# Pooled attention and MLP on one core: pooling of the first group on TensorE, smaller pieces of w_in, gelu over two blocks

## The chip, the cores and the metric

The kernel runs on one core of one Trainium2 chip. The metric is device time in microseconds (us) of one execution. A core has five engines, each with its own queue that it works off in order: TensorE (PE, matmuls and transposes into PSUM; its weight loads are shown as PEld), VectorE (DVE), ScalarE (ACT), GpSimd (POOL) and SyncE (SP, which here issues the loads and stores). PSUM holds what PE writes.

## The reference

```python
q, k, v: (8, 8, 576, 64)            # batch, heads, tokens, head_dim
k_p = k.reshape(B, H, 72, 8, 64).mean(axis=3)     # 8 tokens pooled into one
v_p = v.reshape(B, H, 72, 8, 64).mean(axis=3)
attn = softmax(q @ k_p.T / sqrt(64))
x = (attn @ v_p).transpose(0, 2, 1, 3).reshape(4608, 512)
h = x @ w_in                         # 512 x 2048
out = gelu_tanh(h) @ w_out           # 2048 x 512
```

## The kernel before, in words

The 4608 rows of x are worked off in nine groups of 512: one for each batch (its first 512 tokens) and one, R, for the last 64 tokens of all eight batches. The order is batches 0 to 6, R, batch 7. A group goes through attention and then the MLP; while PE runs one group's MLP, the attention of the next is slipped in between its matmuls.

**Layout.** K and V of a batch are 9 chunks of 128 pooled rows (`NB`): chunks 0 to 3 are K, chunk 4 is half K and half V, 5 to 8 are V. `pool` (L122) adds 8 float rows in three DVE instructions; `dup_k` (L139) writes the K result twice side by side. `pool_v_pe` (L132) does the sum on PE instead, as eight matmuls with a float identity accumulated in PSUM, and a copy. `k_transpose_pe` and `k_spread` (L171, L181) bring pooled K into `kbd`, block-diagonal by pairs of heads; `spread_v` (L143) multiplies pooled V by a mask into `vbd`. q is cast to bf16 (`cast_q`), transposed four head pairs at a time into `qT` (`q_transpose_pe`, L190).

**A block.** A group has four blocks j of 128 rows. `scores` (L202) makes 8 x 72 scores of a block in a "sc" tile, `exps` (L218) takes the exponential on ACT, `norm` (L225) sums, inverts and multiplies into `eb`; `e_transpose_pe` or a DMA transpose brings it into `eT`, and `values` / `values_half` (L259, L249) give xT. In group R each row belongs to another batch in its half of 64 rows, so `scores` uses two matmuls per head pair there, each for 64 rows of output.

**MLP.** `hidden` (L292) does one block of 128 hidden columns: 4 matmuls over k (`KO`), then a gelu on ACT into `gT`. `output` (L300) is one matmul of the second product; 16 (`FO`) make one 128-row block of the result, which `finish` copies and stores. In `mlp` a hidden block has all 512 rows; in `mlp_first`, for group 0, it has 256 (`half`), so that the work can begin with two blocks of attention done.

**Order.** Everything is written out by hand: an engine's queue has the order of the program text. The runner `hook(s)` calls functions at step s of an MLP; a step is one matmul (0 to 63, or 0 to 127 in `mlp_first`, for w_in; then 64 for w_out). The start, L361 to L471, is straight text: loads on SP, warm-up matmuls on PE (`warm_up`, L407), then pooling, scores, values of blocks 0 and 1 and scores of 2 and 3. Weights land as float in slots of the three-slot pool `kvp` that K and V use as well, and are cast to bf16 (`cast_w_in`, `cast_w_out`). PSUM tiles come from two rings, "mm" (4 of one bank) and "sc" (2 of two banks); a new tile waits until the reader of the one before it in its place is done.

Of the kernel before, what the change touches and what calls it, by code (L numbers as in the profile page):

```python
# [19 lines left out]
def kernel(  # L20
# [55 lines left out]
    def copy(eng, out, in_):  # L76
        if eng is nc.scalar:
            eng.copy(out=out, in_=in_)  # L78
        else:
            eng.tensor_copy(out=out, in_=in_)  # L80
# [41 lines left out]
    def pool(b, c0, c1):  # L122
        if "kvb" not in st[b]:
            st[b]["kvb"] = work.tile([128, NB, 2, D], BF16, name="kvb")
        t = st[b]["kv"][:, c0:c1]
        kvb = st[b]["kvb"]
        add = nc.vector.tensor_tensor
        add(out=t[:, :, 0:4, :], in0=t[:, :, 0:4, :], in1=t[:, :, 4:8, :], op=ALU.add)  # L128
        add(out=t[:, :, 0:2, :], in0=t[:, :, 0:2, :], in1=t[:, :, 2:4, :], op=ALU.add)  # L129
        add(out=kvb[:, c0:c1, 0, :], in0=t[:, :, 0, :], in1=t[:, :, 1, :], op=ALU.add)  # L130

    def pool_v_pe(b, c0, c1, eng):  # L132

        ps = psum.tile([128, 2, D], F32, name="vp", tag="mm", bufs=4)
        for i in range(8):
            nc.tensor.matmul(out=ps, lhsT=identf, rhs=st[b]["kv"][:, c0:c1, i, :], start=(i == 0), stop=(i == 7))
        copy(eng, st[b]["kvb"][:, c0:c1, 0, :], ps)

    def dup_k(b, c0, c1):  # L139
        kvb = st[b]["kvb"]  # L140
        nc.vector.tensor_copy(out=kvb[:, c0:c1, 1, :], in_=kvb[:, c0:c1, 0, :])
# [60 lines left out]
    def scores(g, j):  # L202
        sc = psum.tile([128, 2, MAIN], F32, name="sc", tag="sc", bufs=2)
        qT = st[g]["qT"]
        for pr in range(HP):
            o = sc[:, pr // 2, 2 * Sp * (pr % 2):2 * Sp * (pr % 2) + 2 * Sp]
            if g < B:
                nc.tensor.matmul(out=o, lhsT=qT[:, j, pr, :], rhs=kbd[:, g, pr].rearrange("d hh s -> d (hh s)"),  # L208
                                 start=True, stop=True)
            else:  # L210
                for half in range(2):
                    p0 = 64 * half
                    nc.tensor.matmul(out=o[p0:p0 + 64], lhsT=qT[:, j, pr, p0:p0 + 64],  # L213
                                     rhs=kbd[:, 2 * j + half, pr].rearrange("d hh s -> d (hh s)"),
                                     start=True, stop=True)
        st[g][("sc", j)] = sc
# [8 lines left out]
    def norm(g, j, eng):  # L225
        e = st[g][("e", j)]
        den = work.tile([128, H], F32, name="den")
        nc.vector.reduce_sum(out=den, in_=e, axis=AX.X)  # L228
        r = work.tile([128, H], F32, name="r")
        nc.vector.reciprocal(out=r, in_=den)  # L230
        eng.tensor_tensor(out=eb[:, j, 128 * 5 - W:].rearrange("p (h s) -> p h s", s=Sp), in0=e,  # L231
                          in1=r.unsqueeze(2).to_broadcast([128, H, Sp]), op=ALU.mult)
# [4 lines left out]
    def e_transpose_pe(g, j, eng):  # L237
        tp = psum.tile([128, 5, 128], BF16, name="tp", tag="mm", bufs=4)
        for c in range(5):
            nc.tensor.transpose(out=tp[:, c, :], in_=eb[:, j, 128 * c:128 * c + 128], identity=identb)  # L240
        copy(eng, st[g]["eT"][:, j], tp)
# [7 lines left out]
    def values_half(g, half, x, eng):  # L249

        xo = psum.tile([128, 2, 256], F32, name="xo", tag="mm", bufs=4)
        for i in range(2):
            pr = 2 * x + i
            for y, (c, n) in enumerate(PARTS[pr]):
                nc.tensor.matmul(out=xo[:, i, :], lhsT=vbd[:, g, n, :],  # L255
                                 rhs=st[g]["eT"][:, 2 * half:2 * half + 2, c, :], start=(y == 0), stop=(y == 1))
        copy(eng, st[g]["xT"][:, 2 * x:2 * x + 2, 256 * half:256 * half + 256], xo)
# [34 lines left out]
    def hidden(g, fo, c0, c1, hook, s):  # L292
        hp = psum.tile([128, MAIN], F32, name="mm", tag="mm", bufs=4)
        for ko in range(KO):
            hook(s + ko)
            nc.tensor.matmul(out=hp[:, 0:c1 - c0], lhsT=w_in_b[:, ko, fo * 128:(fo + 1) * 128],  # L296
                             rhs=st[g]["xT"][:, ko, c0:c1], start=(ko == 0), stop=(ko == KO - 1))
        nc.scalar.activation(out=gT[:, fo, c0:c1], in_=hp[:, 0:c1 - c0], func=ACT.Gelu_apprx_tanh)  # L298
# [10 lines left out]
    def mlp(g, hooks, last):  # L309
        hook = runner(hooks)  # L310
        for fo in range(FO):
            hidden(g, fo, 0, MAIN, hook, 4 * fo)
# [22 lines left out]
    def mlp_first(g, hooks):  # L335
# [3 lines left out]
        for half, c in [(0, 0), (0, 1), (0, 2), (0, 3), (1, 0), (1, 1), (1, 2), (1, 3)]:  # L339
            for fo in range(4 * c, 4 * c + 4):  # L340
                hidden(g, fo, 256 * half, 256 * half + 256, hook, s)
                s += 4
# [30 lines left out]
    for c in range(2):  # L373
        t = kvp.tile([128, KO, 1024], F32, name="w_in_s", tag="kv")
        w_in_s.append(t)
        for i in range(2):
            nc.sync.dma_start(
                out=t[:, :, 512 * i:512 * i + 512],
                in_=moe_w_in[:, 1024 * c + 512 * i:1024 * c + 512 * i + 512].rearrange("(ko p) f -> p ko f", p=128))

    def cast_w_in(c, eng):
        o = 512 * c
        copy(eng, w_in_b[:, :, o:o + 512], w_in_s[c // 2][:, :, 512 * (c % 2):512 * (c % 2) + 512])
# [9 lines left out]
    def cast_w_out(c, eng):  # L393
        copy(eng, w_out_b[:, 4 * c:4 * c + 4, :], w_out_s[c // 2][:, 4 * (c % 2):4 * (c % 2) + 4, :])

    make_identity(nc, identb)
    nc.vector.memset(kbd, 0.0)
# [7 lines left out]
    make_identity(nc, identf)  # L405
# [7 lines left out]
    warm_up(44, "mm")  # L413
    kT_tile(0, "mm")
    pool(0, 0, 2)
    dup_k(0, 0, 2)
    k_transpose_pe(0, 0, 2)
    pool(0, 2, 4)
    dup_k(0, 2, 4)
    warm_up(22, "mm")  # L420
    k_transpose_pe(0, 2, 4)
    pool(0, 4, 5)
    dup_k(0, 4, 5)
    warm_up(22, "mm")
    k_transpose_pe(0, 4, 5)
    k_spread(0, [nc.vector, nc.scalar])
# [3 lines left out]
    warm_up(12, "mm")  # L430
# [3 lines left out]
    q_transpose_pe(0, 1, nc.scalar, "mm")  # L434
    warm_up(4, "sc")
# [3 lines left out]
    pool(0, 5, 7)  # L439
    spread_v(0, nc.gpsimd, (0,))  # L440
    pool_v_pe(0, 7, 9, nc.scalar)
    spread_v(0, nc.gpsimd, (1,))
    cast_q(0, 2, 4, nc.gpsimd)
    spread_v(0, nc.gpsimd, (2,))
    warm_up(8, "mm")
    norm(0, 0, nc.vector)
    norm(0, 1, nc.vector)
    e_transpose_pe(0, 0, nc.scalar)
    q_transpose_pe(0, 2, nc.scalar, "mm")
    q_transpose_pe(0, 3, nc.scalar, "mm")  # L450
    e_transpose_pe(0, 1, nc.vector)
    cast_w_in(0, nc.vector)
    scores(0, 2)
    exps(0, 2)
    values_half(0, 0, 0, nc.vector)
    scores(0, 3)
    exps(0, 3)
    values_half(0, 0, 1, nc.scalar)
    nc.scalar.preload_act_table_set(GELU_SET)
    norm(0, 2, nc.gpsimd)  # L460
    cast_w_in(1, nc.vector)
    norm(0, 3, nc.vector)
    cast_w_in(2, nc.gpsimd)

    def first_t(j):
        e_transpose_pe(0, j, nc.vector)

    def first_v():
        cast_w_in(3, nc.vector)
        values_half(0, 1, 0, nc.scalar)  # L470
        values_half(0, 1, 1, nc.vector)  # L471
# [10 lines left out]
    load_main(1, "v", 0, 4, nc.sync)  # L482
# [10 lines left out]
    def at(hooks, s, f, *a):  # L493
        hooks.setdefault(s, []).append(lambda: f(*a))  # L494
# [7 lines left out]
    hooks = {}  # L502
    at(hooks, 16, first_t, 2)
    at(hooks, 32, first_t, 3)
    at(hooks, 42, first_v)
    at(hooks, 66, pool, 1, 0, 4)
    at(hooks, 66, dup_k, 1, 0, 4)
    at(hooks, 66, pool, 1, 4, 5)
    at(hooks, 66, dup_k, 1, 4, 5)
    at(hooks, 80, cast_q, 1, 0, 2, nc.vector)  # L510
    at(hooks, 80, cast_q, 1, 2, 4, nc.vector)
    at(hooks, 96, kT_tile, 1, "sc")
    at(hooks, 96, qT_tile, 1)
    at(hooks, 96, k_transpose_pe, 1, 0, 5)
    at(hooks, 96, k_spread, 1, [nc.vector, nc.vector])
    for j in range(4):
        at(hooks, 104 + 6 * j, q_transpose_pe, 1, j, nc.vector, "sc")
    at(hooks, 122, eT_tile, 1)
    at(hooks, 122, cast_w_out, 0, nc.vector)
    at(hooks, 122, cast_w_out, 1, nc.gpsimd)  # L520
    for j in range(4):
        at(hooks, [126, 127, 136, 140][j], scores, 1, j)
        at(hooks, [128, 128, 136, 140][j], exps, 1, j)
        at(hooks, [136, 140, 144, 148][j], norm, 1, j, nc.vector)
        at(hooks, [136, 140, 144, 148][j], e_transpose_dma, 1, j)
    at(hooks, 141, cast_w_out, 2, nc.scalar)
    at(hooks, 141, cast_w_out, 3, nc.scalar)
# [3 lines left out]
    at(hooks, 150, q_tile, 2)  # L531
    at(hooks, 150, load_q, 2, 0, 4, nc.sync)
    at(hooks, 150, load_kv, 2)
    tail_of_attention(hooks, 1, 187)
    mlp_first(0, hooks)

    for n_, g in enumerate(seq):
# [3 lines left out]
        if n_ + 1 < len(seq):  # L541
# [7 lines left out]
            if kv:  # L549
                t0 = 20 if n_ == 1 else 12  # L550
# [59 lines left out]
```

The softmax here doesn't subtract the row's maximum and nothing guards it: scores larger than these inputs give would overflow.

## Time and profile before

| what | value |
|---|---|
| median of 3 runs | 301.0 us (301.0 to 301.05) |
| profiled execution | 301.36 us, its span 299.3 us |
| PE busy | 290.7 us, 97% of the span, 1734 matmuls |
| ACT, DVE, POOL busy | 158.2, 146.7, 55.5 us |
| matmuls on w_out (L301) / on w_in (L296) | 128.6 / 127.6 us |
| gelu (L298) | 88.4 us in 160 instructions |
| K landed, first 512 KB | 4.20 us |
| first matmul on w_in / on w_out | 19.26 / 38.70 us |
| DMA engines, busy share from 5 to 45 us | 1.05 to 1.10 |

How to read the profile: times are from the start of the span. An instruction group has a line (L80 and L78 are the helper `copy` on DVE and ACT, so the tile's name tells what is copied), engine, operation, out<-in, shape and count. A bracket such as `[0.51 <-DMA w_in_s]` is the idle time of the engine just before, and what ended it. Matmuls are pipelined: a group's time runs from its first start to its last end. "The chain" follows the work that ended last back to the start; its last column is us, what. An engine's busy share over the span says little about the first 40 us, which differ from the rest.

### The profile page before, as it was taken

What the parts mean: (1) busy time and instruction counts of PE and PEld (TensorE: products, weight loads), DVE (VectorE), ACT (ScalarE), POOL (GpSimd) and SP (SyncE); (2) the same over time, 40 slices, a digit from 0 to 9 for tenths busy, and PEclk for the clock granted to TensorE, in tenths of its full rate; (3) what the DMA queues carried; (4) which work ended last, traced back from release to release, by engine and by line L of the source; (5) the groups of instructions that cost most, each with busy time, mean ns of one, the idle gap of its engine ahead of it and who ended that gap; (6) DMA issues with size and microseconds to landing.
All of it is one profiled execution on the core that took longest, in us unless ns stands there. A gap on an engine that the chain in (4) does not pass through costs nothing.

```text
span 299.3 us, 4581 instructions
## 1 busy us (share of the span) xinstructions
PE 290.7 (97%) x1734; PEld 151.6 (51%) x1734; DVE 146.7 (49%) x241; ACT 158.2 (53%) x242; POOL 55.5 (19%) x71
## 2 busy tenths in 40 slices
PE   7869999999999999999999999999999999999996
PEld 7748844445444544454445444544444544444444
DVE  6895769164706570648073807381639100920012
ACT  1477783667157715672477246724773267426500
POOL 3252033230400240024012400240024000100000
PEclk9999999999999999999999999999999999999999
DMA  7999997995699459947993599049944800351012
GB/s 235 357 387 338 384 350 132 343 279 158 135 279 250 145 127 271 269 146 126 261 297 134 119 249 301 4 107 249 276 147 101 164 36 2 79 114 37 0 70 70
DMA packets 73221, 56.32 MB, mean 188 GB/s; under 512 B 45808, under 2 KB 55408, under 8 KB 73200
## 3 DMA queue, kind: packets, MB, share of 16 engines
q1 hardware_dynamic: 73056, 55.98, 68.2%
q8 instruction: 13, 0.21, 0.3%
q10 hardware_dynamic: 144, 0.07, 0.1%
q14 instruction: 8, 0.07, 0.1%
HBM read 36.70 MB, written 9.44 MB: 154 GB/s over the span
## 4 chain that ended last, share of the span: by engine, by line
PE 91%; DMA 3%; DVE 2%; SPq 1%; POOL 1%; issue 0%; POOLq 0%
PE mm L296 41%; PE mm L301 41%; PE xo L266 4%; DMA q_sb<-in_q_dram 3%; PE sc L208 2%; PE mm L329 1%; POOL eb L231 1%; SPq L98 1%; PE xo L272 1%; PE tp L193 1%; PE sc L213 0%; DVE w_in_b L80 0%; PE tp L240 0%; DVE w_out_b L80 0%; POOL q_b L80 0%; PE xo L255 0%
## 5 line engine op out<-in xcount | busy, mean ns | idle before, releaser
L301 PE MATMUL mm<-w_out_b,gT 128*128 128x512 bf16 x560 | 128.6, 379 | 0.5 <-DVE w_out_b L80 0.5
L296 PE MATMUL mm<-xT,w_in_b 128*128 128x512 bf16 (+1 forms) x640 | 127.6, 358 | 0.5 <-DVE xT L80 0.5
L298 ACT ACTIVATE gT<-mm 128x512 bf16<-128x512 f32 (+1 forms) x160 | 88.4, 555 | 47.0 <-PE mm L296 45.9
L296 PEld LDWEIGHTS <-w_in_b 128*128 128x128 bf16 x640 | 62.2, 98 | 62.6 <-issue 0.5
L301 PEld LDWEIGHTS <-gT 128*128 128x128 bf16 x560 | 53.4, 98 | 59.7 <-DVE w_out_b L80 0.7
L80 DVE COPY osb<-mm 128x512 f32<-128x512 f32 (+2 forms) x37 | 24.3, 658 | 62.9 <-PE mm L301 60.8
L78 ACT CAST xT<-xo 128x1024 bf16<-128x1024 f32 (+1 forms) x18 | 16.6, 966 | 56.8 <-PE xo L266 49.1
L228 DVE TENSOR_REDUCE den<-e 128x8 f32<-128x576 f32 x36 | 26.5, 736 | 38.0 <-ACT e L221 37.9
L148 POOL TENSOR_TENSOR vbd<-kvb,vmask 128x256 bf16<-128x256 bf16 (+2 forms) x40 | 21.2, 553 | 113.5 <-DVE kvb L130 113.4
L128 DVE TENSOR_TENSOR kv<-kv 128x1024 f32<-128x1024 f32 (+3 forms) x20 | 22.4, 1118 | 29.7 <-DMA kv<-in_v_dram 27.7
L231 DVE TENSOR_TENSOR eb<-e,r 128x576 bf16<-128x576 f32 x28 | 27.2, 970 | 1.0
L221 ACT ACTIVATE e<-sc 128x576 f32<-128x576 f32 x36 | 22.5, 650 | 9.6 <-ACT e L221 4.0
L231 POOL TENSOR_TENSOR eb<-e,r 128x576 bf16<-128x576 f32 x8 | 10.1, 1266 | 71.5 <-ACT e L221 41.1
L80 POOL CAST q_b<-q_sb 128x2048 bf16<-128x2048 f32 (+1 forms) x7 | 15.0, 2147 | 4.1 <-DMA q_sb<-in_q_dram 4.1
L208 PEld LDWEIGHTS <-qT 128*128 128x128 bf16 x128 | 10.1, 98 | 7.0 <-ACT qT L78 0.6
L208 PE MATMUL sc<-kbd,qT 128*128 128x144 bf16 x128 | 13.2, 226 | 0.2 <-ACT qT L78 0.2
L266 PE MATMUL xo<-eT,vbd 128*128 128x512 bf16 x56 | 13.2, 379 | 0.0
L129 DVE TENSOR_TENSOR kv<-kv 128x512 f32<-128x512 f32 (+3 forms) x20 | 12.8, 640 | 0.7
L410 PE MATMUL warm<-identb 128*128 128x128 bf16 x112 | 9.1, 249 | 1.4 <-POOL vmask L398 1.4
L494 ACT ACT_TABLE_LOAD x8 | 10.3, 1283 | 0.1
L80 DVE COPY kbd<-kTd 64x288 bf16<-64x288 bf16 x12 | 5.6, 467 | 8.3 <-DMA kTd<-kvb 8.2
L314 ACT ACT_TABLE_LOAD x7 | 9.0, 1283 | 0.1
(55 smaller groups left out, 99.5 us busy)
## 6 DMA issues: line engine op xcount, KB each, us to landing
out_dram<-osb SPq DMA_DIRECT2D x31, 256.0 KB, 6.7
kv<-in_k_dram SPq DMA_DIRECT2D x7, 1024.0 KB, 6.5
q_sb<-in_q_dram SPq DMA_DIRECT2D x7, 1024.0 KB, 5.9
kv<-in_v_dram SPq DMA_DIRECT2D x7, 1024.0 KB, 9.9
w_in_s<-in_moe_w_in_dram SPq DMA_DIRECT2D x4, 1024.0 KB, 13.0
w_out_s<-in_moe_w_out_dram SPq DMA_DIRECT2D x4, 1024.0 KB, 13.8
out_dram<-osb SPq DMA_DIRECT2D x9, 128.0 KB, 2.3
kv<-in_k_dram SPq DMA_DIRECT2D x2, 512.0 KB, 3.9
```

What stands on the lines that cost most here:

```text
L78: eng.copy(out=out, in_=in_)
L80: eng.tensor_copy(out=out, in_=in_)
L128: add(out=t[:, :, 0:4, :], in0=t[:, :, 0:4, :], in1=t[:, :, 4:8, :], op=ALU.add)
L148: eng.tensor_tensor(out=vbd[p0:128, b, n0:n1, :].rearrange("p (c r) (hh d) -> p c (r hh) d", c=max(m, 1), d=D), in0=kvb[p0:128, 4 + c0:4 + ...
L208: nc.tensor.matmul(out=o, lhsT=qT[:, j, pr, :], rhs=kbd[:, g, pr].rearrange("d hh s -> d (hh s)"), start=True, stop=True)
L221: nc.scalar.activation(out=e.rearrange("p (x h) s -> p x (h s)", x=2), in_=sc[:, :, 0:4 * Sp], func=ACT.Exp, scale=1.0 / 64.0)
L228: nc.vector.reduce_sum(out=den, in_=e, axis=AX.X)
L231: eng.tensor_tensor(out=eb[:, j, 128 * 5 - W:].rearrange("p (h s) -> p h s", s=Sp), in0=e, in1=r.unsqueeze(2).to_broadcast([128, H, Sp]), ...
L266: nc.tensor.matmul(out=xo[:, i, :], lhsT=vbd[:, g, n, :], rhs=eT[:, :, c, :], start=(x == 0), stop=(x == 1))
L296: nc.tensor.matmul(out=hp[:, 0:c1 - c0], lhsT=w_in_b[:, ko, fo * 128:(fo + 1) * 128], rhs=st[g]["xT"][:, ko, c0:c1], start=(ko == 0), stop ...
L298: nc.scalar.activation(out=gT[:, fo, c0:c1], in_=hp[:, 0:c1 - c0], func=ACT.Gelu_apprx_tanh)
L301: nc.tensor.matmul(out=o, lhsT=gT[:, fo, r * 128:(r + 1) * 128], rhs=w_out_b[:, fo, :], start=(fo == 0), stop=(fo == FO - 1))
```

## The change

Seven things, in the order of the program:

1. K of group 0: chunks 0, 1 and 4 are pooled on PE (`pool_pe`, which now does one or two chunks and writes the result once or twice), chunks 2 and 3 on DVE. V chunks 5 to 8 are all pooled on PE; before, 5 and 6 were on DVE. The float identity is made right after the bf16 one. Warm-ups are 40, 8 and 14 instead of 44, 22, 22, 12, 4 and 8.
2. In the start, the q casts of blocks 2 and 3, the transposes and the copies change engine and order; block 3's scores move to step 4 of the MLP, block 2's norm goes from GpSimd to DVE. `values_half` copies each of its two parts on an engine of its own.
3. w_in is loaded in eight pieces of 512 KB (two of the four k) instead of four of 1 MB; seven casts are on GpSimd and one on DVE, where before three were on DVE and one on GpSimd.
4. `hidden_half` does two hidden blocks of 256 rows in one PSUM tile with one gelu; the order of column quarters is half 0: 0, 1, 2, half 1: 0, then 3 of half 0, and the rest of half 1.
5. w_out is cast in nine pieces, five on GpSimd and four on ACT, instead of one on DVE, one on GpSimd and two on ACT.
6. The steps of group 1's attention move to later ones, and V of batch 1 is loaded in two pieces.
7. In group R, scores use 64x64 tiles of PE: each matmul takes one head's 64 rows of K and 64 rows of output, 72 columns. Its heads lie in another order in the tile, and `norm` puts them back.

```diff
-    def pool_v_pe(b, c0, c1, eng):
+    def pool_pe(b, c0, c1, copies, eng):
+        n = c1 - c0
         ps = psum.tile([128, 2, D], F32, name="vp", tag="mm", bufs=4)
         for i in range(8):
-            nc.tensor.matmul(out=ps, lhsT=identf, rhs=st[b]["kv"][:, c0:c1, i, :], ...)
-        copy(eng, st[b]["kvb"][:, c0:c1, 0, :], ps)
+            nc.tensor.matmul(out=ps[:, 0:n], lhsT=identf, rhs=st[b]["kv"][:, c0:c1, i, :], ...)
+        copy(eng, kvb[:, c0:c1, 0:copies, :], ps[:, 0:n].unsqueeze(2).to_broadcast([128, n, copies, D]))
...
+            for hh in range(2):
+                for p0 in (0, 64):
+                    h0 = 64 * hh
+                    nc.tensor.matmul(out=sc[p0:p0 + 64, hh, Sp * pr:Sp * pr + Sp],
+                                     lhsT=qT[h0:h0 + 64, j, pr, p0:p0 + 64],
+                                     rhs=kbd[h0:h0 + 64, 2 * j + p0 // 64, pr, hh], start=True, stop=True)
...
+    def hidden_half(g, fo, half, hook, s):
+        c0 = 256 * half
+        hp = psum.tile([128, 2, 256], F32, name="mm", tag="mm", bufs=4)
+        for f in range(2):
+            for ko in range(KO):
+                hook(s + 4 * f + ko)
+                nc.tensor.matmul(out=hp[:, f, :], lhsT=w_in_b[:, ko, (fo + f) * 128:(fo + f + 1) * 128],
+                                 rhs=st[g]["xT"][:, ko, c0:c0 + 256], start=(ko == 0), stop=(ko == KO - 1))
+        nc.scalar.activation(out=gT[:, fo:fo + 2, c0:c0 + 256], in_=hp, func=ACT.Gelu_apprx_tanh)
...
-        for half, c in [(0, 0), (0, 1), (0, 2), (0, 3), (1, 0), (1, 1), (1, 2), (1, 3)]:
+        for half, c in [(0, 0), (0, 1), (0, 2), (1, 0), (0, 3), (1, 1), (1, 2), (1, 3)]:
...
+    warm_up(40, "mm")
+    pool_pe(0, 0, 2, 2, nc.scalar)
+    kT_tile(0, "mm")
+    pool(0, 2, 4)
+    dup_k(0, 2, 4)
+    warm_up(8, "sc")
+    k_transpose_pe(0, 0, 2)
+    pool_pe(0, 4, 5, 2, nc.scalar)
+    k_transpose_pe(0, 2, 4)
+    k_transpose_pe(0, 4, 5)
+    k_spread(0, [nc.vector, nc.scalar])
+    warm_up(14, "sc")
     cast_q(0, 0, 1, nc.vector)
     cast_q(0, 1, 2, nc.scalar)
     q_transpose_pe(0, 0, nc.vector, "mm")
-    q_transpose_pe(0, 1, nc.scalar, "mm")
+    q_transpose_pe(0, 1, nc.vector, "mm")
     for j in range(2):
         scores(0, j)
         exps(0, j)
+    pool_pe(0, 5, 7, 1, nc.scalar)
+    spread_v(0, nc.gpsimd, (0, 1))
+    pool_pe(0, 7, 9, 1, nc.scalar)
     spread_v(0, nc.gpsimd, (2,))
     norm(0, 0, nc.vector)
     norm(0, 1, nc.vector)
+    e_transpose_pe(0, 0, nc.scalar, "mm")
+    cast_q(0, 2, 3, nc.scalar)
+    cast_q(0, 3, 4, nc.gpsimd)
+    cast_w_in(0, 0, nc.gpsimd)
+    e_transpose_pe(0, 1, nc.vector, "mm")
     q_transpose_pe(0, 2, nc.scalar, "mm")
+    q_transpose_pe(0, 3, nc.scalar, "sc")
+    for x in range(2):
+        values_half(0, 0, x, [nc.vector, nc.scalar], "mm")
     scores(0, 2)
     exps(0, 2)
+    cast_w_in(0, 2, nc.vector)
+    norm(0, 2, nc.vector)
+    for c in range(1, 4):
+        cast_w_in(c, 0, nc.gpsimd)
+        cast_w_in(c, 2, nc.gpsimd)
...
+    at(hooks, 4, scores, 0, 3)
+    at(hooks, 4, exps, 0, 3)
+    at(hooks, 4, nc.scalar.preload_act_table_set, GELU_SET)
+    at(hooks, 4, norm, 0, 3, nc.vector)
     at(hooks, 16, first_t, 2)
     at(hooks, 32, first_t, 3)
-    at(hooks, 42, first_v)
+    at(hooks, 38, first_v)
...
-    at(hooks, 80, cast_q, 1, 0, 2, nc.vector)
+    at(hooks, 80, cast_q, 1, 0, 2, nc.gpsimd)
...
+    at(hooks, 110, cast_w_out, 0, 1, nc.gpsimd)
+    at(hooks, 110, cast_w_out, 1, 2, nc.gpsimd)
+    at(hooks, 110, cast_w_out, 2, 4, nc.gpsimd)
+    at(hooks, 110, cast_w_out, 4, 6, nc.gpsimd)
+    at(hooks, 110, cast_w_out, 6, 8, nc.gpsimd)
...
-        at(hooks, [126, 127, 136, 140][j], scores, 1, j)
-        at(hooks, [128, 128, 136, 140][j], exps, 1, j)
-        at(hooks, [136, 140, 144, 148][j], norm, 1, j, nc.vector)
+        at(hooks, [128, 131, 142, 146][j], scores, 1, j)
+        at(hooks, [128, 131, 142, 146][j], exps, 1, j)
+        at(hooks, [142, 146, 150, 154][j], norm, 1, j, nc.vector)
...
+    for f in range(8, 16, 2):
+        at(hooks, 147, cast_w_out, f, f + 2, nc.scalar)
...
-    tail_of_attention(hooks, 1, 187)
+    tail_of_attention(hooks, 1, 188)
```

## The prediction

> **What bounds the kernel now.** I read the page first, then the chain of work that ended last in order of time, the timeline of the first 56 us, and the waits.
>
> On the page, TensorE (PE) is what to look at: apart from the first four slices it is busy throughout. A change can only pay by letting this stream start earlier, by closing a hole in it, or by taking work out of it.
>
> ```profile
> ## 2 busy tenths in 40 slices
> PE   7869999999999999999999999999999999999996
> ```
>
> The chain shows where the stream is still thin (columns: start us, us, what). Up to 14.65 it is a load: the second half of q. Then come hand-offs between engines, until PE sits behind a GpSimd (POOL) instruction and transposes its result at 22.38. After that nearly every piece is PE's, but for a short wait for the first cast of w_out ahead of 38.70.
>
> ```profile
> 4.84 9.81 DMA q_sb<-in_q_dram
> 14.65 0.05 issue
> 14.70 1.05 POOL q_b L80
> ...
> 20.25 2.09 POOL eb L231
> 22.34 0.05 issue
> 22.38 0.45 PE tp L240 x5
> ...
> 37.51 1.15 DVE w_out_b L80
> 38.65 0.05 issue
> 38.70 1.90 PE mm L301 x8
> ```
>
> The waits put a price on both holes (engine, line, who it waited for, us in total, times, longest):
>
> ```profile
> PE tp L240 <- POOL eb L231: 1.2, 1, 1.2
> PE mm L301 <- DVE w_out_b L80: 0.5, 1, 0.5
> ```
>
> So from 22.38 on the stretch to the end is PE work and one hole of 0.5. My yardstick is the start of that transpose of block 2's weights (call it the **mark**, 22.38 now): same place in PE's order in both kernels, after the first 16 matmuls on w_in.
>
> The timeline has the prices I need. Columns: start, us from first start to last end, engine, line, count.
>
> ```profile
> 1.43 4.45 PE L410 MATMUL warm<-identb 128*128 128x128 bf16 x44 [1.43 <-POOL vmask L398]
> ...
> 12.01 2.00 PE L136 MATMUL vp<-kv,identf 128*128 128x128 f32 x16
> ...
> 14.05 0.27 ACT L78 CAST kvb<-vp 128x128 bf16<-128x128 f32 x1 [1.18 <-PE vp L136]
> ...
> 15.06 1.29 DVE L231 TENSOR_TENSOR eb<-e,r 128x576 bf16<-128x576 f32 x1
> ...
> 22.83 1.93 POOL L80 CAST w_in_b<-w_in_s 128x2048 bf16<-128x2048 f32 x1 [0.51 <-DMA w_in_s<-in_moe_w_in_dram]
> ```
>
> Eight float matmuls of the pooling are 16 PE passes; a pass is in flight 0.275, so they start (2.00 - 0.275)/15 = 0.115 apart. One pooling of two chunks costs PE 1.84 and gives its result after 2.00. VectorE (DVE) does the same two chunks in 1.71 (0.69 + 0.42 + 0.29 + 0.20 and gaps, 4.20 to 5.91).
>
> **What the Trainium skill says.** "TensorE: Matmul & The Clock Gate", Part 1: matmuls of 128 columns start 107 ns apart until the clock opens after about 3.4 us of work, then 56. The trace agrees: 44 starts in 4.45 - 0.23 fit 36 at 107 and 7 at 56, so the clock opens near 5.25. Same page, "LDWEIGHTS": a load takes columns/1.2 ns, 107 for 128; the trace's 115 ns per pass fits both this and the streaming, so it doesn't say what a pass of 64 columns costs. "SBUF — State Buffer", "Who interferes with whom": a DVE instruction with two SBUF inputs and a GpSimd instruction that reads SBUF block each other. The trace agrees in direction: the multiply above took 1.29 beside a GpSimd product, 0.76 to 0.82 elsewhere. "TensorEngine Tiling (Array Packing)", "Key Properties": changing the tiling mode drains TensorE, and tiles run independently; see the last group below.
>
> **The change, part by part.** All times on the profiled execution's own axis (span 299.3; its run took 301.36, so 2.06 lies around the span, and the median of the runs is 301.0, 0.36 less; I add the difference to the median).
>
> *K of the first group.* PE now pools chunks 0-1, behind 40 warm-ups: 36 at 107 and 4 at 56 ns from 1.43 leave PE free at 5.49, although K landed at 4.20. Pooling 5.52 to 7.52; ScalarE (ACT) copy with the doubling, 0.27 for 128 elements plus about 0.1 for 128 more (its 128x256 and 128x512 gelus differ by 0.21): 7.93. Then two transposes, and the pooling of chunk 4 as 16 passes of 64 columns from 8.12. Unknown price: 0.115 each if the weight load sets the pace, half if streaming does. I take the load: 8.12 + 15 x 0.115 + 0.25 = 10.10; copy to 10.41; last K transpose ends 10.66. Before, 9.02 + 0.20 = 9.22. Chunks 2-3 stay on DVE and are done near 7.3, beside this. So **K is 1.44 later**; the lower bound is 0.6 later.
>
> *To the scores.* From that transpose to the second block's scores took 9.22 to 11.75 = 2.53; a qT copy moves from ACT (0.59) to DVE (0.43): 2.37, so 13.03. The clock has no say: the q for this landed before 9.48.
>
> *V on PE.* Right behind, first pass at 13.03 + 0.26 = 13.29 (the distance now is 12.01 - 11.75). 32 passes: 31 x 0.115 + 0.275 = 3.84, **end 17.13**; now the 16 end at 14.01. DVE is relieved of 1.4 (10.72 to 12.18), but it was not the last to arrive.
>
> *ACT's queue up to the first hidden matmul.* After the V passes ACT runs in order: V copy 0.27, eT copy 0.69, q cast 0.62, then (PE transposes q, 0.40) two qT copies 1.07, two quarter xT copies of 0.37. With hand-offs of 0.02 to 0.05: 17.13 + 3.96 = 21.09. The exp behind it, 0.65, ends 21.74. Meanwhile GpSimd has its products (1.0), q cast (0.5, half of 1.04) and w_in pieces at 0.97 (half of 1.93); the first ends near 20.1, DVE's own piece (0.63) at 21.3 to 21.8, so hidden starts near 21.2 instead of 19.26. w_in has landed long before (its third MB at 22.83, loads 2.7 apart, so the first near 17.4): the finer pieces gain nothing here.
>
> *Mark.* The norm of block 2 moves from GpSimd (2.08) to DVE: 0.74 + 0.20 + 0.76 and gaps = 1.82 from 21.74: 23.56. GpSimd is then casting w_in piece after piece; half of the seen excess (1.29 - 0.76) is 0.27. PE at 23.88: **+1.50**. That wait has 112 hidden matmuls queued behind it, and ACT's gelus wait for those. Bounds: -0.3 without contention, +0.3 with all of it.
>
> *After the mark.* The wait for w_out goes: **-0.50**. GpSimd casts it in pieces from hook 110, near 35.5 (512 elements 0.5); the first MB was landed by 37.4 at the latest and PE needs it near 39.4. Next late would be GpSimd's pieces of the second MB, landed 38.06, needed 16 matmuls in. Two score blocks of group 1 move across the first output matmul, and one of group 0 across the hidden start: PE work kept. Norm of block 3 follows on DVE (1.75) within the 16 matmuls (1.76) that PE runs meanwhile: 0 to 0.3, taken 0.
>
> *At nothing.* A gelu over two blocks: 0.60 for eight matmuls (0.87) instead of two of 0.385: ACT waits for PE there in both; without that cover 0.17 per pair was to win. w_in in 8 loads instead of 4 and V of group 1 in 2 instead of 1: five more DMA issues on SP, whose queue in that stretch is held back by full DMA engines (1.05 of a share from 5 to 45 us); behind them stand the loads of group 1, w_out and then the transposes of eb near 43, so bytes land in the same order. Later hooks for group 1 and t0 = 26: DVE's four norms and two V poolings end about 14.0 after the first output matmul, PE asks for them 14.0 (first half of the heads: 13.0) after it, as now (13.7 and 13.4). w_out on ACT in four halves: same elements, 3.7. The norm of group R writes the same 576 elements.
>
> *Scores of group R.* Now 8 passes of 144 columns per block on two column tiles:
>
> ```profile
> 221.26 0.44 PE L213 MATMUL sc<-kbd,qT 128*64 128x144 bf16 x8
> ```
>
> On the chain a block takes 0.37, and the outputs behind it 0.11 more than in other groups; a plain block 0.25. So 0.24 of work (30 ns per pass: two at a time) and 0.23 of draining. Its eight weight loads start (0.27 - 0.11)/7 = 23 ns apart. After: 16 loads and passes of 72 columns. At 23 ns each 0.37, which is 0.13 more, times 4: **+0.50**. Bounds: four truly at once, 16 x 30/4 = 0.12, so -0.5; 30 ns each, +1.0.
>
> **Sum:** +1.50 - 0.50 + 0.50 = **+1.5**: 302.9 on the profiled execution, 302.5 on the median.
>
> **The rivals.**
> *Half-price chunk 4.* If 64 columns cost 57 ns a pass, everything from 10.10 on is 0.86 earlier: 301.7. For it: 128 columns also fit streaming. Against: the fp32 loads are 192 ns in flight, bf16 ones 98.
> *Four tiles at once.* R's blocks take 0.12 instead of 0.37: 4 x 0.25 = 1.0 less, 301.5. For it: the two column tiles do run in pairs. Against: the loads at 23 ns.
> *The hand-offs overlap: faster.* If ACT's queue doesn't set the start, PE's own order does: 13.03 + 0.26 + 32 x 0.115 = 16.97, then 0.56 + 0.44 + 0.86 + 0.25 of transposes, values and scores: hidden at 19.1, mark at 19.1 + 1.76 + 0.25 = 21.1, so -1.3 - 0.5 + 0.5: 299.7. It decides from where the last xT copy ends before about 19.6 (19.6 + 0.65 + 1.82 + 0.05 + 0.27 puts the mark at 22.4, where the sum is nought). For it: in the 5.20 us ahead of hidden ACT is busy for only 3.60 now. Against: the order of ACT's queue is written out, and the q cast stands behind the eT copy.
> *Cold pooling.* If the clock opens after the first pooling instead of before it, its passes cost up to twice 107 ns, 0.1 more each: +1.6, 304.1. The 40 warm-ups end only 0.25 after the change of clock.
> That the change doesn't do what it says is no rival for the pooling; for "as they land" it is part of my forecast.
>
> **How the numbers follow.** Forecast 0.52, chunk 4 at half price 0.15, four tiles 0.12, hand-offs 0.11, cold 0.10. About 0.2% (0.6 us) is what a measurement of this kernel can tell from no change, so same is 300.4 to 301.6. Faster: the hand-offs, 0.11. Same: four tiles most of it, half of chunk 4's case and a little of the forecast's low end, 0.20. Slower: the rest, 0.69. The forecast's own spread is 301.7 to 303.7 (contention 0.3, block 3's wait 0.3, R 0.5). For 8 in 10 the range reaches over half price and four tiles and part of the cold case: 300.8 to 303.9.
>
> **What would show it.** K's last transpose ending near 10.7 (9.8 for half price); V passes ending near 17.1; the last xT copy of the first half near 21.1; the mark near 23.9; no wait ahead of the first output matmul; R's blocks 0.5 on the chain. Wrong if the mark is at or before 22.4: then my ACT chain or the pass price is too long.

## The result, and the profile after

The changed kernel takes 304.62 us (median of four runs, 303.54 to 304.79) where the one before took 301.02: ratio 1.0107 (1.0081 to 1.0134), so it is slower, by more than twice what was forecast, and above the range. Measured again later it took 304.85 against 301.25: 1.0114 (1.0101 to 1.0128). The profiled execution took 304.79, its span is 303.1; before, 301.36 and 299.3.

The page of the changed kernel, busy tenths of PE in slices of 7.6 us: the first and the third have gained one, the fourth (22.7 to 30.3 us) has lost two. After that nothing differs.

```profile
## 2 busy tenths in 40 slices
PE   8877999999999999999999999999999999999996
```

PE's waits (engine, line, who it waited for, us in total, times, longest). The wait for w_out is gone, as forecast. The first line is new, and the prediction has nothing of it:

```profile
PE xo L269 <- DVE xT L80: 2.1, 4, 0.5
PE tp L254 <- DVE eb L240: 0.8, 2, 0.5
```

The chain of work that ended last, in order of time (start us, us, what). Where the prediction had two ACT copies of 0.37 behind the q transposes, PE and DVE take turns: two matmuls, a copy, then matmuls again, a copy. The mark is the transpose that follows at 25.82 (ahead of it stands block 2's multiply, 24.47 to 25.76).

```profile
14.25 3.63 PE vp L140 x32
17.91 0.27 ACT kvb L78
18.19 0.69 ACT eT L78
18.88 0.53 ACT q_b L78
19.45 0.78 PE tp L198 x8
20.23 0.23 PE xo L269 x2
20.48 0.43 DVE xT L80
20.96 0.61 PE xo L269 x4
21.60 0.43 DVE xT L80
22.07 0.39 PE xo L269 x2
22.49 0.37 ACT xT L78
```

The timeline of the changed kernel (start, us from first start to last end, engine, line, count) has the prices of the new pooling:

```profile
1.43 4.45 PE L437 MATMUL warm<-identb 128*128 128x128 bf16 x40 [1.43 <-POOL identb masks.py:199]
...
5.67 2.68 PE L140 MATMUL vp<-kv,identf 128*128 128x128 f32 x16
...
8.94 1.95 PE L140 MATMUL vp<-kv,identf 128*128 128x64 f32 x16
...
14.09 3.78 PE L140 MATMUL vp<-kv,identf 128*128 128x128 f32 x32
```

All 40 warm-ups ran 107 ns apart (39 x 0.107 + 0.23 = 4.40), and the first pooling took 2.68 instead of 2.00: the clock opened only in the middle of it, near 7.1 by my reckoning from these two lines.

The time divides as follows, by three landmarks (the mark, the first hidden matmul of group 1, the last copy of the result):

| stretch | before | after | difference | forecast |
|---|---|---|---|---|
| to the mark | 22.38 | 25.82 | +3.44 | +1.50 |
| mark to group 1's first hidden matmul | 32.73 | 33.63 | +0.90 | -0.50 |
| from there to the last copy | 241.26 | 240.82 | -0.44 | +0.50 |
| sum | 296.37 | 300.27 | +3.90 | +1.5 |

### The profile page after: what moved, and what is told of

Same layout as the page of the kernel before. It is cut to its first block, busy times and chain, and to the rows that moved or that the text cites. A ratio compares the mean times of both kernels' runs of the same rounds, so it can differ in the third digit from the quotient of the medians.

```text
span 303.1 us, 4608 instructions
## 1 busy us (share of the span) xinstructions
PE 292.0 (96%) x1738; PEld 154.7 (51%) x1764; DVE 141.2 (47%) x230; ACT 156.9 (52%) x233; POOL 62.9 (21%) x81
## 4 chain that ended last, share of the span: by engine, by line
PE 94%; DVE 2%; ACT 2%; issue 1%; POOL 0%; POOLq 0%; ACTq 0%
PE mm L326 40%; PE mm L310 36%; PE xo L280 4%; PE mm L321 3%; PE vp L140 3%; PE sc L213 3%; PE warm L437 2%; PE mm L354 1%; DVE eb L240 1%; PE xo L269 1%; PE tp L198 1%; PE xo L286 1%; DVE xT L80 1%; DVE den L235 0%; ACT gT L312 0%
## 5 line engine op out<-in xcount | busy, mean ns | idle before, releaser
L326 PE MATMUL mm<-w_out_b,gT 128*128 128x512 bf16 x542 | 126.1, 379 | 1.1 <-issue 0.3
L310 PE MATMUL mm<-xT,w_in_b 128*128 128x512 bf16 x504 | 111.4, 379 | 0.4
L312 ACT ACTIVATE gT<-mm 128x512 bf16<-128x512 f32 x128 | 76.3, 597 | 41.9 <-PE mm L310 41.9
L153 POOL TENSOR_TENSOR vbd<-kvb,vmask 128x256 bf16<-128x256 bf16 (+2 forms) x40 | 21.3, 555 | 122.4 <-DVE kvb L133 109.9
L131 DVE TENSOR_TENSOR kv<-kv 128x1024 f32<-128x1024 f32 (+3 forms) x17 | 20.7, 1220 | 31.6 <-DMA kv<-in_v_dram 29.0
L240 DVE TENSOR_TENSOR eb<-e,r 128x576 bf16<-128x576 f32 x26 | 25.3, 973 | 1.1 <-DVE r L237 0.3
L240 POOL TENSOR_TENSOR eb<-e,r 128x576 bf16<-128x576 f32 x6 | 6.9, 1150 | 60.5 <-ACT e L228 33.3
L80 POOL CAST q_b<-q_sb 128x2048 bf16<-128x2048 f32 (+2 forms) x8 | 16.2, 2020 | 7.8 <-DMA q_sb<-in_q_dram 7.8
L321 PE MATMUL mm<-xT,w_in_b 128*128 128x256 bf16 x128 | 15.8, 273 | 0.4 <-DVE w_in_b L80 0.4
L132 DVE TENSOR_TENSOR kv<-kv 128x512 f32<-128x512 f32 (+3 forms) x17 | 11.7, 685 | 0.6
L323 ACT ACTIVATE gT<-mm 128x512 bf16<-128x512 f32 x16 | 9.4, 597 | 4.7 <-PE mm L321 4.6
```

What stands on the lines that cost most here:

```text
L153: eng.tensor_tensor(out=vbd[p0:128, b, n0:n1, :].rearrange("p (c r) (hh d) -> p c (r hh) d", c=max(m, 1), d=D), in0=kvb[p0:128, 4 + c0:4 + ...
L240: eng.tensor_tensor(out=o.rearrange("p (h s) -> p h s", s=Sp), in0=e, in1=r.unsqueeze(2).to_broadcast([128, H, Sp]), op=ALU.mult)
L310: nc.tensor.matmul(out=hp, lhsT=w_in_b[:, ko, fo * 128:(fo + 1) * 128], rhs=st[g]["xT"][:, ko, :], start=(ko == 0), stop=(ko == KO - 1))
L312: nc.scalar.activation(out=gT[:, fo, :], in_=hp, func=ACT.Gelu_apprx_tanh)
L321: nc.tensor.matmul(out=hp[:, f, :], lhsT=w_in_b[:, ko, (fo + f) * 128:(fo + f + 1) * 128], rhs=st[g]["xT"][:, ko, c0:c0 + 256], start=(ko ...
L326: nc.tensor.matmul(out=o, lhsT=gT[:, fo, r * 128:(r + 1) * 128], rhs=w_out_b[:, fo, :], start=(fo == 0), stop=(fo == FO - 1))
```

## The experiments

Eleven variants ran, and the changed kernel again, each timed against the one before on the same chip. I began with **theory A**: `values_half` in the changed kernel issues the copy of a head pair directly behind its two matmuls, and both pairs lie in one PSUM tile, so the second pair's matmuls wait until the first copy is done. Against it stood what I had priced myself: late K, a late clock, contention with GpSimd.

### Both copies behind all four products

```diff
-            copy(engs[i], st[g]["xT"][:, pr, 256 * half:256 * half + 256], xo[:, i, :])
+        for i in range(2):
+            copy(engs[i], st[g]["xT"][:, 2 * x + i, 256 * half:256 * half + 256], xo[:, i, :])
```

> The changed kernel, but the two copies of a values tile are issued behind all four products of the tile instead of each behind its own two. Theory A (the second pair of products waits for the copy of the first pair, because both lie in one PSUM tile): the four waits of about 0.67 us between products go, the last xT copy of the first half ends near 21.7 instead of 22.86, the second half takes 0.9 instead of 2.2, and the time falls by 2 to 2.7 us to about 302.2. Rival B (the pooling on TensorE and the ScalarE queue set the mark, and the products wait there in any case): the mark stays near 25.8, at most 1 us is won.

Measured: 301.63 (301.02 to 302.77), ratio 1.0018 (1.0011 to 1.0025). Two lines moved take back 3.0 of the 3.6 us. In its timeline the eight products of a half are one piece of 1.04, and no wait at L269 is left:

```profile
19.16 1.04 PE L269 MATMUL xo<-eT,vbd 128*128 128x256 bf16 x8
...
23.93 0.45 PE L254 MATMUL tp<-identb,eb 128*128 128x128 bf16 x5 [0.54 <-DVE eb L240]
```

V's passes end at 16.96 (forecast 17.13), the last copy at 21.07 (21.09), the mark stands at 23.93 (23.88). With the copies late, the prediction's times for the start hold almost line by line. Theory A stands; not all of the 3.0 is its own (see the repeat below).

The split itself gains nothing even so. The same timeline shows ACT idle until DVE's copy of the tile is done:

```profile
19.80 0.86 DVE L80 CAST xT<-xo 128x256 bf16<-128x256 f32 x2 [1.75 <-PE xo L269]
...
20.26 0.81 ACT L78 CAST xT<-xo 128x256 bf16<-128x256 f32 x2 [0.20 <-DVE xT L80]
```

All four of ACT's copies in this trace begin 0.03 after DVE's copy of the same tile ends. The last copy ends 0.87 after the last product; in the kernel before, with one whole copy per tile on an engine of its own, 0.73.

### The same two copies alone, in the kernel before

```diff
-        copy(eng, st[g]["xT"][:, 2 * x:2 * x + 2, 256 * half:256 * half + 256], xo)
+            copy([nc.vector, nc.scalar][i], st[g]["xT"][:, pr, 256 * half:256 * half + 256], xo[:, i, :])
```

> The kernel before, with the two copies of a values tile split and each issued behind its own two products, nothing else. Theory A: each of four tiles makes TensorE wait 0.5 to 0.7 us, part of it hidden in the first half where it waits anyway: 1.0 to 2.4 us slower, 302.0 to 303.4. Rival B: split copies are shorter (0.42 and 0.37 instead of 0.68 and 0.58), so the time stays within 0.4 us of 301.0 or falls.

Measured: 303.69 (303.0 to 304.34), ratio 1.0081 (1.0068 to 1.0094), +2.6. The waits of this kernel show the same line, and two of the four waits are longer, since DVE's copies there sit behind w_in casts:

```profile
PE xo L255 <- DVE xT L80: 2.9, 4, 1.2
```

Not all of the 2.6 is these waits. In the profiled run TensorE's granted clock was at half from 20.0 to 23.4 us (PEclk on the page is that clock, in tenths, over the same 40 slices), and the first 16 hidden matmuls took 3.35, where they take 1.93 in the kernel before:

```profile
PEclk9989999999999999999999999999999999999999
```

```profile
20.50 3.35 PE L296 MATMUL mm<-xT,w_in_b 128*128 128x256 bf16 x16
```

Over the whole run its granted clock was 0.994; so it was in two more of the five runs. The other two, at 1.0, took 303.0 and 303.09. So by these two runs the edit alone costs about 2.0, and 2.6 with what the clock adds in most runs. What lowered the clock isn't shown.

### Group R's 64x64 tiles alone, in the kernel before

The edit is the scores' part of the diff above and the norm that puts the heads back in order.

> The kernel before, with only group R's scores on 64x64 tiles and the norm that puts the heads back. Reading of the changed kernel's trace (four tiles at once, 0.25 instead of 0.37 on the chain): 0.5 us faster, 300.5. The prediction's price (16 loads 23 ns apart): 0.5 slower, 301.5.

Measured: 300.66 (300.37 to 301.04), ratio 0.9985 (0.9979 to 0.9991): 0.4 faster. I had taken +0.50. On the chain of the kernel before, a block of R's scores is

```profile
221.33 0.37 PE sc L213 x8
```

and on that of the changed kernel

```profile
225.70 0.25 PE sc L220 x16
```

Twice the passes in 0.12 less, and as much as a plain block takes (0.25); four blocks make 0.48. The cycle from R's first hidden matmul to the next group's is 31.41 before and 30.93 in the changed kernel. The single matmuls in the trace show why: the 16 passes start four at a time, 0.003 apart (at 225.63, 225.68, 225.71 and 225.75), the 8 of before two at a time. The outputs behind the first block still take 0.54 for two. The four tiles run at once: the rival had it right.

### K back on VectorE, and then with the late copies

```diff
-    warm_up(40, "mm")
-    pool_pe(0, 0, 2, 2, nc.scalar)
+    warm_up(44, "mm")
+    pool(0, 0, 2)
+    dup_k(0, 0, 2)
...
-    pool_pe(0, 4, 5, 2, nc.scalar)
+    pool(0, 4, 5)
+    dup_k(0, 4, 5)
```

The fillers between the transposes go back to 22, 22 and 12. With the changed kernel's copies:

> The changed kernel with K of the first group pooled on VectorE again and the warm-ups there as before (44, 22, 22, 12); V stays on TensorE. Theory: K's last transpose ends near 9.2 instead of 11.45 and all up to the mark moves with it, 2.2 us earlier: 302.4. Rival: the second half of q (landed near 14.7) or the pieces of w_in come late next, and under 1 us is won. If the clock of TensorE opens near 5.3 here and near 7 in the changed kernel, 0.8 of the 2.2 is the clock's.

Measured: 302.09 (301.53 to 302.78), ratio 1.0033 (1.0021 to 1.0045), 2.5 less than the changed kernel. In the traces K's last transpose ends 1.14 earlier than in the changed kernel with an early clock (see the repeat below: 9.14 against 10.28), and block 2's multiply starts between two casts and takes 0.76 instead of 1.29; the mark is 1.68 earlier (22.97 against 24.65), and the rest of the 2.5 these traces don't show. The four waits at L269 are there as before (2.1 in all). With the late copies as well:

> The changed kernel with both undone: values copies behind all products of their tile, and K of the first group on VectorE with the old warm-ups. If the two costs are apart (each sits on the path by itself): 302.1 less 2.4 to 3.0, or 301.6 less 1.3 to 2.5, so 299.2 to 300.2, faster than both kernels. If they hide each other, or group 1's later attention comes late next: 300.8 to 301.6.

Measured: **300.17** (300.09 to 300.29), ratio 0.9967 (0.9955 to 0.9979): faster than both kernels (the best kernel from here on). K on PE thus costs 1.46 beside late copies (301.63 to 300.17; about 1.5 by the ratios), where I had put its lateness at 1.44. It is no pure lateness, though, so that the two figures are so close is partly luck. The last K transpose ends 1.20 earlier than in the first experiment (9.34 against 10.54), the mark comes 0.91 earlier (23.02 against 23.93), and the first w_out matmul 1.38 earlier (38.38 against 39.76): the multiplies of blocks 2 and 3 meet GpSimd's casts at another moment, 1.49 and 0.76 here, 1.20 and 1.56 there.

What this best kernel has over the one before: the mark is 0.64 later, the stretch to group 1 takes 0.92 less (0.50 of it the wait for w_out; 0.16 one score block that no longer waits; the rest I did not trace), and group R 0.44 less. The smaller pieces of w_in, the finer casts of w_out and the later steps of group 1 are in it; none of them was undone alone.

### Half of V back on VectorE

From the best kernel, `pool(0, 5, 7)` in place of `pool_pe(0, 5, 7, 1, nc.scalar)`.

> As the one before (late copies, K on VectorE), and V chunks 5 and 6 of the first group on VectorE as well, as in the kernel before. Theory (pooling V on TensorE holds up what stands behind it on TensorE and ScalarE): TensorE's passes end 1.8 us earlier, the mark 0.5 to 1.3 us earlier, the time falls by as much. Rival (VectorE's norms come 1.4 us later and set the mark then): within 0.3 us of the one before, or slower.

Measured: 301.65 (300.52 to 302.56), ratio 1.0018 (1.0008 to 1.0027), slower than with all of V on PE. The waits up to 30 us show why the gain doesn't come:

```profile
PE tp L254 <- DVE eb L240: 3.2, 3, 1.5
```

DVE, which pools first, begins its norm of block 0 at 13.31 instead of 12.17, and PE, spared 1.9 of passes, waits for it. The mark and the first w_out matmul (23.08, 38.44) are as in the best kernel within 0.06. In the profiled run another 0.44 is lost near 70 us, where the chain leaves PE for the next batch's K:

```profile
64.53 4.47 DMA kTd<-kvb
...
69.65 0.41 PE sc L213 x4
```

So V on PE is not what makes the change slow. The median is 1.5 above the best kernel's, where the traces show 0.5; the granted clock of the single runs accounts for most of the rest. The four runs at 1.0, the profiled one among them, took 300.52 to 301.17. The other thirteen were at 0.994 or 0.988 and took 301.32 to 302.56. None of those thirteen has a trace, so where their clock fell isn't shown.

### The warm-ups: 56 and 26 instead of 40

Both on top of the late copies, to see what the late clock costs.

> The changed kernel with late copies (301.6, single runs 301.0 to 302.8) and 56 warm-ups instead of 40. Theory (the clock opens at another moment in each run, and a pooling that begins before it pays up to 0.8 us): the spread of single runs shrinks to under 1 us, the first pooling takes 2.00 in the profile and starts about 0.9 later, the median rises by 0.2 to 0.9. Rival (the spread comes from elsewhere, loads for instance): the spread stays near 1.7.

> The changed kernel with late copies (301.6) and 26 warm-ups instead of 40, so that TensorE is free for the first pooling near 4.2, when K lands. Theory (a pass costs 0.115 with the clock open, twice 0.107 before that; the clock opens 3 to 6 us after the first matmul, differently from run to run): the 16 passes begin near 4.25, take 2.4 to 3.5 and end between 6.6 and 7.8, against 7.4 with 40 warm-ups and an early clock and 8.35 with a late one; the median falls by 0 to 0.6. Rival (a cold pass costs more, or fewer warm-ups open the clock later): slower than 301.6.

Measured: 302.87 (301.94 to 303.48), ratio 1.0053 (1.0041 to 1.0066) with 56; 302.06 (301.65 to 302.57), ratio 1.0028 (1.0017 to 1.004) with 26. With 56 the first pooling starts at 6.87 and the mark is at 25.35, 1.42 later than with 40; these six runs still spread over 1.5, so an early pooling isn't what spreads them. With 26 the pooling ran from 4.32 for 2.17, and the mark came 0.79 earlier (23.14); yet there is no gain. In its profiled run 0.47 is lost again by the end, in one group where PE's values had to wait, up to 143.64. What they waited for the profile doesn't name; that group's cycle is 30.83 where the others take 30.35. Neither count is better than 40.

### Gelu over two blocks alone, in the kernel before

```diff
-            for fo in range(4 * c, 4 * c + 4):
-                hidden(g, fo, 256 * half, 256 * half + 256, hook, s)
-                s += 4
+            for fo in range(4 * c, 4 * c + 4, 2):
+                hidden_half(g, fo, half, hook, s)
+                s += 8
```

> The kernel before with only the gelus of the first group over two blocks of 128 (one of 0.60 for two of 0.385). The prediction put this at nothing, since ScalarE waits for TensorE there: within 0.3 us of 301.0. Rival (ScalarE sets the pace at 0.43 per gelu against 0.44 of TensorE, and the last gelus delay the exponentials): 0.3 to 0.8 faster; or slower by as much, if the first gelu comes too late for its tile's next use.

Measured: 301.52 (301.2 to 301.95), ratio 1.0012 (1.0005 to 1.0018), +0.33, where I had costed it at nothing. The last gelu takes 0.60 instead of 0.38 and the exps of group 1 stand behind it on ACT. From this kernel's timeline:

```profile
38.21 0.60 ACT L309 ACTIVATE gT<-mm 128x512 bf16<-128x512 f32 x1 [1.00 <-PE mm L307]
...
40.12 1.19 ACT L221 ACTIVATE e<-sc 128x576 f32<-128x576 f32 x2
...
40.82 0.41 PE sc L208 x4
```

The scores start at 40.82, in the kernel before at 40.63: 0.19 of the 0.33. In the changed kernel no score block waits there, so the cost isn't in its sum.

### One w_in piece cast by VectorE

Two attempts to clear the multiplies of contention, from the best kernel: first the second half (k 2 and 3) of quarter 1 moved from GpSimd to DVE, behind block 2's norm; then in addition the same half of quarter 0 moved the other way.

```diff
-    for c in range(1, 4):
+    cast_w_in(1, 0, nc.gpsimd)
+    cast_w_in(1, 2, nc.vector)
+    for c in range(2, 4):
```

> The kernel with late copies and K on VectorE (300.2), and one piece of w_in (second quarter, second half of k) cast by VectorE behind block 2's norm instead of by GpSimd beside it. Theory (the norm's multiply, 1.49 there and 0.76 alone, is held up by GpSimd's cast): the multiply takes 0.8 to 0.9, the mark comes 0.5 to 0.7 earlier than 23.02, of which 0.2 to 0.3 is lost at block 3's transpose: 299.6 to 299.9. Rival (the mark's wait is hidden by something else that comes as late): within 0.2 of 300.2, or slower through the 0.65 that VectorE now casts.

> As the one before, and the first quarter's second piece goes from VectorE to GpSimd, which has it done near 19.6 instead of 20.2 if the pieces are behind each other there. Theory: TensorE's wait for w_in (0.5) goes as well, but the mark is set by exp and norm, so at most 0.2 more than the one before: 299.4 to 299.9. Rival: GpSimd's later pieces move by 1.0 and one of them meets the norm again: 300.2.

Measured: 301.41 (301.13 to 301.98), ratio 1.0007 (0.9999 to 1.0016), and 301.47 (301.06 to 304.4), ratio 1.0025 (1.0011 to 1.0038). The second kernel's runs lie in two groups with a gap from 301.6 to 302.57; eight of the nine in the upper group had a granted clock of 0.994, all of the lower one 0.999 or 1.0. Misses, both. The timeline of the first:

```profile
21.32 1.04 POOL L80 CAST w_in_b<-w_in_s 128x1024 bf16<-128x1024 f32 x1 [1.68 <-DMA w_in_s<-in_moe_w_in_dram]
21.44 1.53 DVE L240 TENSOR_TENSOR eb<-e,r 128x576 bf16<-128x576 f32 x1
22.68 4.33 POOL L80 CAST w_in_b<-w_in_s 128x1024 bf16<-128x1024 f32 x3 [0.31 <-DMA w_in_s<-in_moe_w_in_dram]
22.89 1.52 DVE L80 CAST w_in_b<-w_in_s 128x1024 bf16<-128x1024 f32 x1
```

GpSimd's casts are paced by landings here, so taking a piece out of its queue doesn't move the next: the one that lands near 21.3 still meets the multiply (1.53). And DVE's own cast beside GpSimd's takes 1.52, where it took 0.81 in the best kernel; PE waits 0.78 for it. In the second kernel the multiply came down to 1.01, and that cast still took 1.52.

The lines above also show a rule that both expectations lacked. GpSimd's cast ends at 21.32 + 1.04 = 22.36, which is 0.92 after the multiply's start; 0.76 + 0.92 - 0.15 = 1.53. In all 14 traces of this case (402 such multiplies on DVE) the multiply takes 0.76 plus what is left, at its start, of the GpSimd instruction then running, less 0.15 (nothing if less than that is left): with 0.40 left 1.01, with 0.59 left 1.20, with 0.68 left 1.29. A GpSimd instruction that starts after it costs it nothing: in the best kernel block 3's multiply starts at 23.89 and the next cast at 24.01, and it takes 0.76. The DVE casts of 128x1024 go the same way: 0.68 with none running, 0.81 with 0.26 left, 1.52 with 0.98 left.

### The changed kernel again

> The changed kernel itself beside the others. If the clock of TensorE opened late by chance in its first profile, this one has the first pooling at 2.0 instead of 2.68 and the mark near 25.0 instead of 25.8, and the run of that profile is near 304.0; the four waits for copies are there in either case, and the median is 303.5 to 304.7. If the late clock belongs to the kernel, the pooling takes 2.7 again.

Measured: 304.85 (303.94 to 305.19), ratio 1.0114 (1.0101 to 1.0128). The profiled run was its fastest, 303.94, and in it the clock opened early:

```profile
1.43 3.91 PE L437 MATMUL warm<-identb 128*128 128x128 bf16 x40 [1.43 <-POOL identb masks.py:199]
...
5.18 2.00 PE L140 MATMUL vp<-kv,identf 128*128 128x128 f32 x16
...
18.89 0.38 PE L269 MATMUL xo<-eT,vbd 128*128 128x256 bf16 x2
```

Every landmark is 1.17 earlier than in the first profile (mark 24.65, first w_out matmul 41.83 against 43.00), and the four waits of 0.52 are there again. So the late clock was the draw of one run; the copies' waits are in both.

## Why the prediction was wrong

The same points in four columns (us from the start of the span):

| | forecast | after | after again | late copies |
|---|---|---|---|---|
| last K transpose ends | 10.66 | 11.45 | 10.28 | 10.54 |
| block 1's scores start | 13.03 | 13.83 | 12.65 | 12.92 |
| V passes end | 17.13 | 17.87 | 16.69 | 16.96 |
| last xT copy of the first half ends | 21.09 | 22.86 | 21.69 | 21.07 |
| mark | 23.88 | 25.82 | 24.65 | 23.93 |
| first w_out matmul | - | 43.00 | 41.83 | 39.76 |

**The step that failed: "two quarter xT copies of 0.37", with hand-offs of 0.02 to 0.05.** I put them into ACT's queue as if the products had been made in one go before, as they were, and read the change of `values_half` as a matter of which engine copies. But the copy moved into the loop: product, copy, product, copy, on one tile. The Trainium skill, "PSUM — Partial Sum Buffer", section "PSUM bank collisions raise a hardware error", says that access is to be guarded by bank, not by address, since PE's writes and another engine's reads of one bank collide even at other columns. The tile is one bank (2 x 256 floats a partition), and the trace agrees with such a guard: the second pair of products starts 0.05 after the copy of the first ends (20.48 + 0.43, then 20.96). It doesn't tell a guard by bank from one by tile: no kernel here put the two halves into banks of their own. Its price, from the two traces with an early clock (after again, less late copies): V's end to the last copy 5.00 instead of 4.11, 0.89; to the mark 0.10 more; mark to the first w_out matmul 17.18 instead of 15.83, 1.35, as the second half goes through the same four steps. Together 2.3; in the kernel before the same edit alone cost 2.6 on the median, about 2.0 without the drop of the clock. I had also left the second half out altogether: the prediction has no line for `first_v`.

**The clock.** The first profile had the late clock. Against the repeat that is 1.17 on every landmark, against the forecast 0.79 (last K transpose at 11.45 instead of 10.66); the rival for it was priced at 1.6 and given 0.10. It is no part of the change's price that can be counted on: the second profile lacks it. What it does to the medians can't be read from runs that have no trace. By the counts of warm-ups that fit at 107 and at 56 ns, the profiles of all kernels put the opening between 4.5 and 7.1 us.

**Right in place and size.** Chunk 4's 16 passes of 64 columns took 1.95 against 2.00 for 128 columns: the columns streamed don't set the pace, and half price falls. That the weight load sets it fits, but no run varied the load. V's passes took 3.78 (3.84 forecast). The wait for w_out went, and nothing took its place.

**Right in size, in part by luck.** From V's end to the last copy it took 4.11 with late copies against 3.96, and with the mark at 23.93 the rival in which the hand-offs overlap (mark at 21.1) falls. But ACT's queue sets only the first part: ACT was done with q at 20.05, and its last two copies then waited for DVE's. K on PE costs 1.46 on the medians (1.44), 0.91 at the mark.

**Too small.** Block 2's multiply beside GpSimd's cast: 0.27 forecast, 0.53 measured (1.29 against 0.76). I had taken half of a seen excess and had put that excess down to a GpSimd product; at 15.06 it was the cast of q that ran (14.70 to 15.74, 0.68 left), and by the rule above it costs what is left of it, not a mean. Block 3's wait, taken at 0 of a possible 0.3: 0.29, since its multiply too met a cast (1.56).

**Wrong in sign.** Group R, +0.50 forecast, -0.4 measured. I carried over the 23 ns between weight loads from a mode with two tiles to one with four. The Trainium skill's "TensorEngine Tiling (Array Packing)", "Key Properties", which the prediction cites for tiles running independently, speaks for the lower bound; I chose the middle. The trace agrees with the page: the passes start four at a time, and a block takes 0.12 less, which is the lower bound's 0.5 over four blocks.

The three errors, on the profiled execution: unpriced waits of 2.3 and the clock's 0.8 above, R's 0.9 below (its forecast less its measurement), come to +2.2; the miss was 3.9 - 1.5 = 2.4. The K transposes, 0.26 earlier in the one early-clock profile than in the other, show how well such sums can close.

## What to carry to other kernels

When an edit splits a copy out of PSUM between two engines, look at where the copies stand in the program: here a copy between two products of one tile made PE wait for it, even though each has columns of its own. All products first, then both copies, loses PE's wait; the two copies of one tile still went one after the other, so the split within a tile gained nothing. Price every function that the diff touches once for every place it is called from. Price a DVE multiply beside GpSimd with what will be left of the GpSimd instruction running when it starts; where the casts wait for loads, the landings decide that, not the place in the queue. And look at each run's granted clock before a difference between medians is explained.

## What the runs showed of the hardware

- Float passes of PE with a 128x128 identity cost the same for 64 columns as for 128: 1.95 and 2.00 for 16.
- Four 64x64 tiles ran at once: 16 passes of 72 columns, started four at a time, took 0.25 on the chain, 8 passes of 144 on two tiles 0.37.
- PE's clock opened at different moments in the profiles of nearly one and the same start: 40 warm-ups took 3.91, 4.18 and 4.45.
- The clock could fall again: to half for 3.4 us in the profile of the split copies, where 16 matmuls took 3.35 instead of 1.93. In the three kernels that had such runs, those with a granted clock of 0.994 or less took 0.7 to 1.4 longer (by the medians) than the others of the same kernel.
- A DVE multiply of 128x576 (0.76) and a DVE cast of 128x1024 (0.68) took longer by what was left of the GpSimd instruction running at their start, less 0.15 and 0.13. One that started later cost nothing.
- Copies by DVE and ACT out of one PSUM tile went one after the other, 0.03 apart.
